# New planner constants in a fused Hyena-and-SwiGLU kernel: block 2's shift taps go to ScalarE, block 3's filter is turned on TensorE, and every engine's order is planned anew

## The chip, the cores and the metric

The kernel runs on one core of one Trainium2 chip. The metric is the device time of one execution in microseconds; the numbers below are medians over runs of the same program. A profile is one more execution, recorded instruction by instruction; its span reaches from the first to the last recorded instruction.

## What is computed

Two layers of the same pair of operators, with weights shared between the layers, on x of 2048 positions by 512 channels in bf16:

```
x = x + A(layernorm(x), k, v);   x = x + B(layernorm(x))     # layer 0
x = x + A(layernorm(x), k, v);   x = x + B(layernorm(x))     # layer 1
A(q, k, v): kv = (sum over j<4 of shift_k[:, j] * k delayed by j) * v
            y  = causal convolution over the 2048 positions of kv with ssm_k, per channel
            return q * (y + ssm_D * kv)
B(x):       (silu(x @ w_gate) * (x @ w_up)) @ w_down          # 512 -> 1792 -> 512
```

The convolution of A depends on k, v and the filters alone, so its result y is the same in both layers and is computed once.

## The kernel before

**Blocks.** The 2048 positions are cut into four blocks of 512 (`NB = 4`); position 4p + r of a block lies on partition p in row r. A block's FFN work is cut into two halves of 256 positions, so there are 16 FFN units, named (layer, block, half): (0,0,0), (0,0,1), (1,0,0), (1,0,1), (0,1,0) and so on to (1,3,1). The convolution is done block by block in the frequency domain: each block of the filter gives a spectrum `H`, `G`, each block of kv a spectrum `X`; products `X[i]*G[j]` are added into `Z[i+j]`, and the inverse of `Z[c]` is `Y[c]`, which block c needs before its layer 0 can begin. Block c therefore needs the products of all blocks up to c.

**One FFN unit (`ffn`).** `zT` holds the normalised input, transposed. For each of 14 chunks of the 1792 columns, TensorE makes a gate and an up product (line 335); two chunks share one PSUM buffer, so a "gate group" or "up group" is eight 256-column matmuls, and there are seven of each in a unit. Four PSUM buffers (`pf`) hold them. ScalarE empties each: SiLU of the gate into `sg` (line 837), a copy of the up into `ht` (line 841). VectorE multiplies the two (line 844), usually two pairs at a time. TensorE then adds the down product into `pd` (line 851, 512 columns, 28 in a unit). At the end ScalarE copies `pd` to `dn` (line 863) and VectorE adds it to x (line 870); units listed in `X_PE` instead add x itself to `pd` by an identity matmul (line 817), and ScalarE writes `pd` straight to x (line 857).

**The step before a unit (`prologue`).** Row statistics come from VectorE's `bn_stats` (lines 706 to 709) or, for the units in `ST1` and `ST2`, from two ScalarE sums per row with `accum_out` (lines 721 and 728, small VectorE steps 724, 732, 734); GpSimd raises the variance to the power -1/2 (`rstd`, line 711 or 736). The normalisation itself is one VectorE `tensor_scalar` per row (line 754) or, for the units in `N_ACT` (the q of A, tile `n`) and `Z_ACT` (the input of B, tile `z`), one ScalarE activation (line 750) behind a small VectorE step (line 743). VectorE then does q*y and x + q*y (lines 776 and 777). Two DMA transposes on SP's queue (line 783) turn `z` into `zT`.

**Convolution steps of one block (`conv`).** The filter block is transposed either on TensorE (`transpose_h`: 16 matmuls with the identity, line 475, and two 1024-column ScalarE copies, line 479) or, for blocks in `H_DMA`, by four ScalarE copies (line 565) and four DMA transposes (line 569). The four shift taps are applied either on TensorE (`shift_mul`: 64 matmuls of 128 columns, four ScalarE copies at line 498, four VectorE products with v at line 499) or, for blocks in `K_ACT`, by `shift_mul_t`: sixteen ScalarE activations with the tap as a per-partition scale (line 578, tiles `ka` and `kc`), three VectorE additions of 2048 columns (line 582), four DMA transposes (line 586) and two VectorE products with v (line 590). The forward transform is eight matmuls with ScalarE copies (line 423) and VectorE butterflies (lines 518 to 531); a product is two VectorE multiplications and one or two additions (lines 635 to 656).

**What sets the order.** Nothing is scheduled by the compiler. `Plan` records each operation with an assumed cost and, where one is given, a due time; `forward` then runs a list schedule over five engines: among the operations that could start first on an engine it takes the one that is due first. The resulting order is written out, engine by engine, and each engine works through its list in that order:

```
key = (max(est, t[e] + self.WAIT[e]), o.due, o.n)
if pick is None or key < pick[0]:
    pick = (key, est, o)
```

FFN operations are due at a place in their unit, counted from `T0` and the list `DUR` of unit lengths; `back` takes `HSL` off the due time of VectorE's steps of the FFN (kind "h") and `ASL` off that of ScalarE's SiLU and copies (kind "a"). Operations of the convolution are due backwards from what needs them, with their costs multiplied by `STRETCH`, and no earlier than `FLOOR`. `SLK` makes the transposes of `z` due earlier. `LOOSE` names the buffer rings whose slots may be handed out in another order than the buffers were declared.

Of the kernel before, what the change touches and what calls it, by code (L numbers as in the profile page):

```python
# [13 lines left out]
ACT = mybir.ActivationFunctionType  # L14
# [2 lines left out]
LN_EPS = 1e-5  # L17

NB = 4
SLK = 8.52  # L20
H_DMA = lambda b: b in {2, 3}
ST1 = lambda l, c, h: (l, c, h) in {(0, 1, 1), (0, 2, 0), (0, 3, 0), (1, 0, 1)}
ST2 = lambda l, c, h: (l, c, h) in {(0, 1, 1), (0, 3, 1), (1, 0, 0)}
ASL = 8.04
K_ACT = lambda b: b in {3}
PASSES = 1
PW = 1.2
PD_ACT, KV_ACT, ST_ACT = True, True, False
HSL = 13.4
Z_ACT = lambda l, c, h: (l, c, h) in {(0, 3, 1), (1, 1, 0), (1, 1, 1)}  # L30
N_ACT = lambda l, c, h: (l, c, h) in {(0, 2, 0), (0, 2, 1), (1, 2, 1), (1, 3, 0), (1, 3, 1)}
Z_DMA = lambda i, j: False
D_DMA = lambda l, c, h: False
X_PE = lambda l, c, h: (l, c, h) in {(0, 3, 1), (1, 1, 0), (1, 2, 0), (1, 3, 1)}
RINGS = {}
T0, FLOOR = 37.71, 9.21
DUR = [20.73, 19.38, 17.95, 16.46, 26.14, 17.1, 26.09, 16.75, 22.3, 20.61, 21.16, 19.35, 17.53, 22.2, 16.85, 27.0]
STRETCH = {1: {"PE": 2.88, "DVE": 1.23, "ACT": 4.33, "POOL": 1.0, "SP": 160.46},
           2: {"PE": 3.08, "DVE": 1.77, "ACT": 1.75, "POOL": 1.0, "SP": 1.07},
           3: {"PE": 3.04, "DVE": 1.08, "ACT": 2.72, "POOL": 1.0, "SP": 1.04}}  # L40
R = 4


# [23 lines left out]
class Plan:  # L67


    LOOSE = ("pc", "ks")  # L70
    WAIT = {"PE": 0.1, "DVE": 0.15, "ACT": 0.1, "POOL": 0.1, "SP": 0.1}
    SAME = {"PE": 0.0, "DVE": 0.06, "ACT": 0.05, "POOL": 0.1, "SP": 0.0}
    CROSS = {"PE": 0.3, "DVE": 0.2, "ACT": 0.25, "POOL": 0.15, "SP": 0.0}
# [60 lines left out]
    def forward(self):  # L134
# [14 lines left out]
        while len(seq) < len(self.ops):  # L149
            best = None  # L150
            for e, cand in ready.items():
                pick = None
                for o in cand:
# [4 lines left out]
                    for b in o.bufs:  # L158
# [4 lines left out]
                        free = sorted(0.0 if s is None else free_at[s] for s in slots[b.ring] if s is None or not todo[s])  # L163
                        if n >= len(free) or (b.ring not in self.LOOSE and qd[heads[b.ring] + n] is not b):
                            ok = False
# [106 lines left out]
def kernel(  # L272
# [192 lines left out]
    def transpose_h(b, ring, order, conv, engs=("ACT",)):  # L465
        hs = new("hs", "hs", [P, R, D], parts=R)
        m = len(engs)
        for r0 in order:
            rows = range(r0, r0 + 2 // m)
            pt = new(ring, "pt", [P, 2 // m, D], BF16)  # L470

            def go(pt=pt, rows=rows):
                for o, r in enumerate(rows):
                    for dt in range(KD):
                        nc.tensor.transpose(pt.t[:, o, dt * P:(dt + 1) * P], hn[b].t[:, dt, r:L:R], ident.t[:])
            add("PE", pe(KD * len(rows), P), go, r=[hn[b], ident], w=[pt], conv=conv, dest=hs)
            sl = slice(rows[0], rows[-1] + 1)
            if engs[order.index(r0) % m] == "ACT":
                add("ACT", act(len(rows) * D), lambda pt=pt, sl=sl: nc.scalar.copy(out=hs.t[:, sl, :], in_=pt.t[:]),
                    r=[pt], w=[(hs, rows)], conv=conv)  # L480
            else:
                add("DVE", tt1(len(rows) * D), lambda pt=pt, sl=sl: nc.vector.tensor_copy(out=hs.t[:, sl, :], in_=pt.t[:]),
                    r=[pt], w=[(hs, rows)], conv=conv)
        return hs
# [50 lines left out]
    def forward4(rows, name, scale, ring, conv):  # L535
        ev = spectrum(name)
        by_residue(rows, ev, scale, ring, ("ACT",), conv)
        return ev
# [8 lines left out]
    def spectrum_h(b, ring="pc"):  # L547
        hs = transpose_h_dma(b) if H_DMA(b) else transpose_h(b, ring, (0, 2), True)
        H[b] = forward4(hs, "H", 2.0 / N, ring, True)
# [11 lines left out]
    def transpose_h_dma(b):  # L561
        hr = new("s8", "hr", [P, R, KD, P], parts=KD)
        hs = new("hs", "hs", [P, R, D], parts=R)
        for dt in range(KD):
            add("ACT", act(D), lambda dt=dt: nc.scalar.copy(
                out=hr.t[:, :, dt], in_=hn[b].t[:, dt, :].rearrange("d (p r) -> d r p", r=R)), r=[hn[b]], w=[(hr, (dt,))],
                conv=True)
        for r in range(R):
            turned[b] = add("SP", 1.25, lambda r=r: nc.sync.dma_start_transpose(
                out=hs.t[:, r].rearrange("p (k f) -> p k f", k=KD), in_=hr.t[:, r]), r=[hr], w=[(hs, (r,))], lat=3.0 if b == 1 else 1.4, conv=True)  # L570
        return hs

    def shift_mul_t(b):

        a, c = new("s8", "ka", [P, 2, R, KD, P], parts=2 * KD), new("s8", "kc", [P, 2, R, KD, P], parts=2 * KD)
        for j, (t, h) in ((3, (a, 0)), (2, (a, 1)), (1, (c, 0)), (0, (c, 1))):
            for dt in range(KD):
                add("ACT", 0.615, lambda j=j, t=t, h=h, dt=dt: nc.scalar.activation(
                    out=t.t[:, h, :, dt], in_=kT[b].t[:, dt, PADL - j:PADL - j + L].rearrange("d (p r) -> d r p", r=R),
                    func=ACT.Copy, scale=tapF.t[:, dt, j:j + 1]), r=[kT[b], tapF], w=[(t, (h * KD + dt,))], conv=True)  # L580
        for t, h in ((a, 1), (c, 0), (c, 1)):
            dve(4 * D, lambda t=t, h=h: nc.vector.tensor_add(out=a.t[:, 0], in0=a.t[:, 0], in1=t.t[:, h]),
                [(t, range(h * KD, h * KD + KD))], [(a, range(KD))], conv=True)
        ks = c
        for r in range(R):
            add("SP", 1.25, lambda r=r: nc.sync.dma_start_transpose(
                out=ks.t[:, 0, r], in_=a.t[:, 0, r]), r=[(a, range(KD))], w=[(c, (r,))], lat=4.0, conv=True)
        for h in range(2):
            sl = slice(2 * h, 2 * h + 2)
            dve(2 * D, lambda sl=sl: nc.vector.tensor_mul(  # L590
                out=vt[b].t[:, sl, :], in0=ks.t[:, 0, sl].rearrange("p r k d -> p r (k d)"), in1=vt[b].t[:, sl, :]),
                [(c, (2 * h, 2 * h + 1))], [(vt[b], (2 * h, 2 * h + 1))], conv=True)

    def spectrum_x(b):
        if K_ACT(b):
            shift_mul_t(b)
        else:
            shift_mul(b, "pc", True, first if b == 1 else ())
        X[b] = butterfly4(forward4(vt[b], f"X{b}", 1.0, "pc", True), True)
# [101 lines left out]
    def ln_stats(c, rows):  # L701
        n = len(rows)
        mv = new("mv", "mv", [P, n, 2], F32, parts=n)
        for o, i in enumerate(rows):
            st = new("st", "bnst", [P, 6], F32)
            add("DVE", 0.6, lambda st=st, i=i: nc.vector.bn_stats(out=st.t[:], in_=xs[c].t[:, i, :]), r=[(xs[c], (i,))], w=[st])  # L706
            add("DVE", 0.09, lambda st=st, o=o: nc.vector.bn_aggr(out=mv.t[:, o, :], in_=st.t[:]), r=[st], w=[(mv, (o,))])
        ve, rstd = new("ve", "ve", [P, n], F32), new("rs", "rstd", [P, n], F32)
        add("DVE", 0.08, lambda: nc.vector.tensor_scalar(out=ve.t[:], in0=mv.t[:, :, 1], scalar1=LN_EPS, scalar2=None,  # L709
                                                         op0=ALU.add), r=[mv], w=[ve])  # L710
        add("POOL", PW, lambda: nc.gpsimd.tensor_tensor(out=rstd.t[:], in0=ve.t[:], in1=nhalf.t[:].to_broadcast((P, n)),  # L711
                                                          op=ALU.pow), r=[ve, nhalf], w=[rstd])
        return mv, rstd
# [46 lines left out]
    def apply_norm(c, h, layer=0):  # L760
        rows = range(HP * h, HP * h + HP)
        st = ln_stats_act(c, rows) if ST1(layer, c, h) else ln_stats(c, rows)
        nmr = shift_of(st, HP) if N_ACT(layer, c, h) else None
        n = new("n", "n", [P, HP, D], parts=HP)
# [4 lines left out]
    def prologue(layer, c, h, on_pe=False):  # L769
# [5 lines left out]
        if not on_pe:  # L775
            dve(HP * D, lambda: nc.vector.tensor_mul(out=n.t[:], in0=n.t[:], in1=y.t[:, sl, :]), [(y, rows)], [n])
            dve(HP * D, lambda: nc.vector.tensor_add(out=x.t[:, sl, :], in0=x.t[:, sl, :], in1=n.t[:]), [n], [(x, rows)])
            st = ln_stats_act(c, rows) if ST2(layer, c, h) else ln_stats(c, rows)
            nmr = shift_of(st, HP) if Z_ACT(layer, c, h) else None
            for o, i in enumerate(rows):  # L780
                z = new("z", "z", [P, D])
                normalise(z, (0,), lambda z=z: z.t[:], c, i, o, st, nmr)
                add("SP", 1.25, lambda z=z, o=o: nc.sync.dma_start_transpose(
                    out=zT.t[:, :, o, :], in_=z.t[:].rearrange("p (k f) -> p k f", k=KD)), r=[z], w=[(zT, (o,))], lat=1.4, slack=SLK)
            return
# [21 lines left out]
    def ffn(unit):  # L807
# [4 lines left out]
        pairs = NF // 2  # L812
        xpe = X_PE(layer, c, h)
        if xpe:
# [157 lines left out]
    for unit in order:  # L972
        start[unit] = t
        t += DUR[order.index(unit)]

# [38 lines left out]

    plan.dues(STRETCH, FLOOR, {u: (start[u], d) for u, d in zip(order, DUR)}, {"h": HSL, "a": ASL})

# [37 lines left out]
```

## Time and profile before

| | us |
|---|---|
| median of 3 runs (357.68 to 358.32) | 358.32 |
| the profiled execution's own time | 358.32 |
| its span | 356.5 |
| TensorE (PE) busy | 347.6 |
| VectorE (DVE) busy | 281.1 |
| ScalarE (ACT) busy | 238.0 |
| GpSimd (POOL) busy | 39.3 |

The profiled execution stands at the median; 1.8 us of it lie outside the span. The granted TensorE clock was 1.00 in every slice. A matmul's busy time overlaps with the next one's, so the cost of an instruction in a packed list is read from the distance between starts in the timeline and not from its mean duration. The same holds, to a smaller degree, for VectorE and ScalarE.

### The profile page before, as it was taken

To read this page: it belongs to the slowest core of one execution; us is meant where nothing else is said; L and a number is where in the kernel's file an instruction comes from. 1 tells how busy PE (TensorE), PEld (TensorE's weight loads), DVE (VectorE), ACT (ScalarE), POOL (GpSimd) and SP (SyncE) were. 2 spreads that over 40 slices of the span, in tenths; PEclk is the share of its full clock that TensorE was granted. 3 is DMA by queue.
4 is the path that set the end of the run, shared out by engine and by line. 5 is a ranking of instruction groups with operands and counts; after the bars stand their busy time and mean duration, and the time that the engine had idled before them with its cause. 6 is when DMAs were issued, how large, how long until landed. Compare 5 with 4: busy or idle time off the path is not lost.

```text
span 356.5 us, 6735 instructions
## 1 busy us (share of the span) xinstructions
PE 347.6 (97%) x2689; PEld 254.4 (71%) x2712; DVE 281.1 (79%) x517; ACT 238.0 (67%) x454; POOL 39.3 (11%) x42
## 2 busy tenths in 40 slices
PE   7999999999999999999999999999999999999996
PEld 6655985867778585868668685858686777768673
DVE  6997999999989999999999999889985323626020
ACT  4587693838878493648878994848484775647352
POOL 1010010130320200111121000201101000101000
PEclk9999999999999999999999999999999999999999
DMA  7999021010241341010311042010103020101000
GB/s 263 306 353 293 2 69 22 0 31 2 45 119 45 63 147 31 0 31 1 79 40 31 1 116 63 2 29 3 31 29 31 30 31 1 31 1 31 30 2 29
DMA packets 37897, 21.98 MB, mean 62 GB/s; under 512 B 29797, under 2 KB 35690, under 8 KB 37866
## 3 DMA queue, kind: packets, MB, share of 16 engines
q1 hardware_dynamic: 37336, 21.03, 22.9%
q10 hardware_dynamic: 530, 0.53, 0.5%
q8 instruction: 21, 0.34, 0.4%
q14 instruction: 10, 0.08, 0.1%
HBM read 12.33 MB, written 2.10 MB: 40 GB/s over the span
## 4 chain that ended last, share of the span: by engine, by line
PE 49%; DVE 35%; ACT 10%; POOL 3%; issue 2%; DMA 1%; ACTq 0%; POOLq 0%; DVEq 0%
PE pf L335 30%; PE pd L851 15%; DVE m L518 4%; DVE ht L844 3%; DVE bnst L706 3%; DVE t L641 3%; DVE t L635 3%; DVE t L651 2%; POOL rstd L736 2%; ACT H L423 2%; DVE Z L656 2%; PE ps L335 2%; PE wm L1020 1%; DVE t L620 1%; DVE Z L648 1%
## 5 line engine op out<-in xcount | busy, mean ns | idle before, releaser
L335 PE MATMUL pf<-zT,wu_sb 128*128 128x256 bf16 x896 | 116.1, 273 | 0.1
L335 PE MATMUL pf<-zT,wg_sb 128*128 128x256 bf16 x896 | 116.1, 273 | 0.0
L335 PEld LDWEIGHTS <-wg_sb 128*128 128x128 bf16 x896 | 87.6, 98 | 18.9 <-issue 0.8
L851 PE MATMUL pd<-wd_sb,ht 128*128 128x512 bf16 x434 | 98.6, 380 | 1.5 <-DVE ht L844 0.8
L335 PEld LDWEIGHTS <-wu_sb 128*128 128x128 bf16 x896 | 87.6, 98 | 11.1
L837 ACT ACTIVATE sg<-pf 128x512 bf16<-128x512 f32 x112 | 68.9, 615 | 18.2 <-PE pf L335 16.7
L851 PEld LDWEIGHTS <-ht 128*128 128x128 bf16 x448 | 43.6, 98 | 49.8 <-DVE ht L844 1.2
L841 ACT CAST ht<-pf 128x512 bf16<-128x512 f32 x112 | 67.3, 601 | 15.0 <-PE pf L335 14.6
L844 DVE TENSOR_TENSOR ht<-ht,sg 128x1024 bf16<-128x1024 bf16 x64 | 39.5, 619 | 25.7 <-ACT ht L841 25.7
L711 POOL TENSOR_TENSOR rstd<-ve,nhalf 128x2 f32<-128x2 f32 x25 | 26.0, 1039 | 203.2 <-DVE ve L709 180.8
L706 DVE BATCH_NORM_STATS2 bnst<-xc 128x6 f32<-128x512 bf16 x50 | 32.5, 685 | 6.2 <-ACT xc L857 5.6
L863 ACT CAST dn<-pd 128x512 bf16<-128x512 f32 x24 | 12.9, 591 | 34.5 <-PE pd L851 34.5
L870 DVE TENSOR_TENSOR xc<-xc,dn 128x1024 bf16<-128x1024 bf16 x12 | 8.2, 686 | 17.8 <-ACT dn L863 17.8
L635 DVE TENSOR_TENSOR t<-X,G 128x2048 bf16<-128x2048 bf16 x18 | 21.9, 1219 | 0.0
L641 DVE TENSOR_TENSOR t<-X,G 128x2048 bf16<-128x2048 bf16 x18 | 21.9, 1217 | 0.0
L736 POOL TENSOR_TENSOR rstd<-ve,nhalf 128x2 f32<-128x2 f32 x7 | 12.0, 1719 | 80.0 <-DVE ve L732 80.0
L423 ACT ACTIVATE X<-ps 128x512 bf16<-128x512 f32 x32 | 18.8, 635 | 1.2 <-PE ps L335 1.1
L423 ACT ACTIVATE H<-ps 128x512 bf16<-128x512 f32 x24 | 13.4, 645 | 4.3 <-PE ps L335 4.3
L656 DVE TENSOR_TENSOR Z<-Z,t 128x2048 bf16<-128x2048 bf16 x12 | 14.7, 1222 | 0.1
L651 DVE TENSOR_TENSOR t<-t,t 128x2048 bf16<-128x2048 bf16 x12 | 14.6, 1221 | 0.1
L335 PE MATMUL ps<-vt,fwd 128*128 128x512 bf16 x54 | 14.4, 380 | 0.1
L335 PEld LDWEIGHTS <-fwd 128*128 128x128 bf16 x96 | 9.3, 98 | 7.2
(95 smaller groups left out, 316.5 us busy)
## 6 DMA issues: line engine op xcount, KB each, us to landing
vt<-in_A_v_dram SPq DMA_DIRECT2D x4, 512.0 KB, 4.6
xc<-in_A_q_dram SPq DMA_DIRECT2D x4, 512.0 KB, 4.8
out_dram<-xc SPq DMA_DIRECT2D x16, 128.0 KB, 1.7
wg_sb<-in_B_w_gate_dram SPq DMA_DIRECT2D x1, 1792.0 KB, 9.2
wu_sb<-in_B_w_up_dram SPq DMA_DIRECT2D x1, 1792.0 KB
wd_sb<-in_B_w_down_dram SPq DMA_DIRECT2D x1, 1792.0 KB, 12.3
hn<-in_A_ssm_k_dram SPq DMA_DIRECT2D x3, 512.0 KB, 7.6
hn<-in_A_ssm_k_dram ACTq DMA_DIRECT2D x1, 512.0 KB, 3.9
```

Source lines behind the costliest of these rows:

```text
L335: nc.tensor.matmul(o, lhsT=lhsT, rhs=rhs, start=(n == 0), stop=(n == len(terms) - 1))
L423: add("ACT", act(D), lambda: nc.scalar.activation(out=view(), in_=ps.t[:], func=ACT.Copy, scale=scale), r=[ps], w=[(buf, keys)], conv=conv)
L635: dve(n * D, lambda t1=t1, part=part: nc.vector.tensor_mul(out=t1.t[:], in0=x.t[:, sl, 0, :], in1=g.t[:, sl, part, :]), [(x, key(slots, (0 ...
L641: dve(n * D, lambda t2=t2, part=part: nc.vector.tensor_mul(out=t2.t[:], in0=x.t[:, sl, 1, :], in1=g.t[:, sl, 1 - part, :]), [(x, key(slots ...
L651: dve(n * D, lambda t1=t1, t2=t2, comb=comb: nc.vector.tensor_tensor(out=t1.t[:], in0=t1.t[:], in1=t2.t[:], op=comb), [t2], [t1], conv=conv)
L656: dve(n * D, lambda t1=t1, part=part: nc.vector.tensor_add(out=z.t[:, sl, part, :], in0=z.t[:, sl, part, :], in1=t1.t[:]), [t1], [zk], con ...
L706: add("DVE", 0.6, lambda st=st, i=i: nc.vector.bn_stats(out=st.t[:], in_=xs[c].t[:, i, :]), r=[(xs[c], (i,))], w=[st])
L711: add("POOL", PW, lambda: nc.gpsimd.tensor_tensor(out=rstd.t[:], in0=ve.t[:], in1=nhalf.t[:].to_broadcast((P, n)), op=ALU.pow), r=[ve, nha ...
L837: add("ACT", act(D), lambda ps=ps, o=o, sg=sg: nc.scalar.activation(out=sg.t[:, o:o + 2, :], in_=ps.t[:], func=ACT.Silu), r=[ps], w=[(sg, ...
L841: add("ACT", act(D), lambda ps=ps, o=o, ht=ht: nc.scalar.copy(out=ht.t[:, o:o + 2, :], in_=ps.t[:]), r=[ps], w=[(ht, (o // 2,))], due=(uni ...
L844: dve(n * W, lambda sg=sg, ht=ht: nc.vector.tensor_mul(out=ht.t[:], in0=ht.t[:], in1=sg.t[:]), [sg], [ht], due=(unit, k / pairs, 0.0, "h"))
L851: nc.tensor.matmul(pds[o].t[:], lhsT=ht.t[:, q, o * P:(o + 1) * P], rhs=wt["d"].t[:, ft, :], start=(ft == 0 and not xpe), stop=(ft == NF - 1))
```

## The change

Only constants change; the functions stay as they are.

```diff
-SLK = 8.52
-H_DMA = lambda b: b in {2, 3}
-ST1 = lambda l, c, h: (l, c, h) in {(0, 1, 1), (0, 2, 0), (0, 3, 0), (1, 0, 1)}
-ST2 = lambda l, c, h: (l, c, h) in {(0, 1, 1), (0, 3, 1), (1, 0, 0)}
-ASL = 8.04
-K_ACT = lambda b: b in {3}
+SLK = 12.82
+H_DMA = lambda b: b in {2}
+ST1 = lambda l, c, h: (l, c, h) in {(0, 3, 0), (0, 3, 1), (1, 0, 1), (1, 1, 0), (1, 1, 1), (1, 3, 0)}
+ST2 = lambda l, c, h: (l, c, h) in {(0, 2, 0), (0, 2, 1), (1, 2, 0)}
+ASL = -36.81
+K_ACT = lambda b: b in {2, 3}
...
-HSL = 13.4
-Z_ACT = lambda l, c, h: (l, c, h) in {(0, 3, 1), (1, 1, 0), (1, 1, 1)}
-N_ACT = lambda l, c, h: (l, c, h) in {(0, 2, 0), (0, 2, 1), (1, 2, 1), (1, 3, 0), (1, 3, 1)}
+HSL = 60.24
+Z_ACT = lambda l, c, h: (l, c, h) in {(0, 1, 0), (0, 1, 1), (0, 2, 0), (1, 0, 0), (1, 0, 1), (1, 2, 0), (1, 2, 1), (1, 3, 0)}
+N_ACT = lambda l, c, h: (l, c, h) in {(0, 3, 0), (1, 0, 0)}
...
-X_PE = lambda l, c, h: (l, c, h) in {(0, 3, 1), (1, 1, 0), (1, 2, 0), (1, 3, 1)}
+X_PE = lambda l, c, h: (l, c, h) in {(0, 1, 0), (0, 2, 1), (0, 3, 0), (1, 0, 1), (1, 3, 1)}
 RINGS = {}
-T0, FLOOR = 37.71, 9.21
-DUR = [20.73, 19.38, 17.95, 16.46, 26.14, 17.1, 26.09, 16.75, 22.3, 20.61, 21.16, 19.35, 17.53, 22.2, 16.85, 27.0]
-STRETCH = {1: {"PE": 2.88, "DVE": 1.23, "ACT": 4.33, "POOL": 1.0, "SP": 160.46},
-           2: {"PE": 3.08, "DVE": 1.77, "ACT": 1.75, "POOL": 1.0, "SP": 1.07},
-           3: {"PE": 3.04, "DVE": 1.08, "ACT": 2.72, "POOL": 1.0, "SP": 1.04}}
+T0, FLOOR = 87.92, 19.78
+DUR = [20.67, 16.0, 19.32, 17.95, 26.57, 16.97, 27.0, 19.26, 27.0, 17.51, 19.02, 23.16, 25.1, 27.0, 18.4, 23.39]
+STRETCH = {1: {"PE": 1.0, "DVE": 1.41, "ACT": 1.84, "POOL": 1.0, "SP": 58.52},
+           2: {"PE": 1.2, "DVE": 1.44, "ACT": 1.78, "POOL": 1.0, "SP": 1.0},
+           3: {"PE": 6.31, "DVE": 1.15, "ACT": 2.46, "POOL": 1.0, "SP": 3.85}}
...
-    LOOSE = ("pc", "ks")
+    LOOSE = ()
```

In the instruction lists of the two programs this comes to the following counts (before to after):

- TensorE: shift matmuls of 128 columns 192 to 128; filter transposes of 128 columns 32 to 48; identity matmuls of 512 columns (line 817) 8 to 10.
- VectorE: additions of 2048 columns at line 582 3 to 6; products with v at line 590 2 to 4 and at line 499 8 to 4; `bn_stats` and its aggregate 50 to 46 each, line 709 25 to 23; lines 724, 732 and 734 7 to 9 each; line 743 8 to 10; normalisations at line 754 48 to 44; additions at line 870 12 to 11.
- ScalarE: taps 16 to 32; copies at line 498 8 to 4, at line 565 8 to 4, of 1024 columns at line 479 2 to 4; sums at lines 721 and 728 14 to 18 each; normalisations at line 750 16 to 20; the copies of `pd` (lines 857 and 863) stay 32 together.
- SP: DMA transposes at line 569 8 to 4 and at line 586 4 to 8. The load of block 2's v now stands behind the first pair of `zT` transposes, and the transposing load of block 3's k (line 367) stands directly ahead of block 2's four transposes at line 586.

The order of the lists is unchanged up to the first shift matmuls of block 1, some 35 us into the execution, and differs from there on. All 64 shift matmuls of block 1 now come before the first gate group. In ScalarE's list block 2's taps stand as ten in a row, then three, then three; block 3's as eleven, two and three (before: eight in a row, then one at a time). The last down matmuls of unit (1,0,1) now stand behind the first gate group of unit (0,1,0).

## The prediction

> **What bounds the kernel now.** First the page's busy table and its slices of time, to see which engine is full where.
>
> ```profile
> PE 347.6 (97%) x2689; PEld 254.4 (71%) x2712; DVE 281.1 (79%) x517; ACT 238.0 (67%) x454; POOL 39.3 (11%) x42
> ...
> PE   7999999999999999999999999999999999999996
> DVE  6997999999989999999999999889985323626020
> ACT  4587693838878493648878994848484775647352
> PEclk9999999999999999999999999999999999999999
> ```
>
> TensorE is full from slice 2 to slice 39, at full clock. VectorE is as full for two thirds of the span and then empties. The same by stretches, columns PE, PEld, DVE, ACT, POOL:
>
> ```profile
> 37.00:230.00 193.00, 191.50 (x1499) 142.51 (x1509) 186.83 (x315) 141.14 (x279) 26.34 (x19) 1.00 0.18 43
> 230.00:280.00 50.00, 49.79 (x361) 35.45 (x363) 38.62 (x74) 29.55 (x58) 5.05 (x6) 1.00 0.13 22
> 280.00:353.00 73.00, 72.79 (x554) 54.23 (x555) 24.36 (x55) 41.92 (x78) 4.06 (x5) 1.00 0.09 19
> ```
>
> Until 230 us two engines are packed at once; after that TensorE alone. Busy time hides idle inside overlapping matmuls, so I read start distances in the timeline, here around block 3's taps:
>
> ```profile
> 195.94 5.99 PE L851 MATMUL pd<-wd_sb,ht 128*128 128x512 bf16 x27
> 197.76 5.41 ACT L578 ACTIVATE ka<-kTb,tapF 128x512 bf16<-128x512 bf16 x8
> 201.77 1.04 PE L335 MATMUL pf<-zT,wg_sb 128*128 128x256 bf16 x8
> 202.64 1.04 PE L335 MATMUL pf<-zT,wu_sb 128*128 128x256 bf16 x8
> 203.05 1.07 ACT L863 CAST dn<-pd 128x512 bf16<-128x512 f32 x2
> 204.39 1.04 PE L335 MATMUL pf<-zT,wu_sb 128*128 128x256 bf16 x8
> 204.66 0.63 ACT L837 ACTIVATE sg<-pf 128x512 bf16<-128x512 f32 x1
> 205.33 1.03 PE L335 MATMUL pf<-zT,wg_sb 128*128 128x256 bf16 x8
> ```
>
> A group of eight costs TensorE 202.64 - 201.77 = 0.87 us (0.109 a matmul), a 512-column matmul 0.216 (28 down matmuls fill 195.72 to 201.77), a 128-column one about 0.056 (16 in 0.9). Its whole list: 1792 x 0.109 + 608 x 0.216 + 308 x 0.056 = 343.9 us, and its last matmul ends at 352.8. So all its waiting is 8.9 us, 6.9 of it before unit (0,0,1) starts at 59.77, where the list sums to 52.9. I call this difference an engine's lag: TensorE's is 7.7 when (1,0,1) starts (101.51) and 8.8 when (0,2,1) starts (220.39) and at the end. Summed likewise, VectorE's lag is 5.2 at (0,0,1)'s z (ends 51.20, list 46.0) and 8.2 at (0,2,0)'s (193.07, list 184.9): 3 us of waiting in 140.
>
> The timeline also shows what a row of taps costs: eight taps hold ScalarE for 203.05 - 197.76 = 5.29 us (0.661 each). The gate group that began at 201.77 is emptied only at 204.66, and the third gate group, which wants its PSUM buffer, starts at 205.33 instead of 205.26. The 28 down matmuls beside the taps were the cover. With two later gaps, block 3's taps cost TensorE 0.36 us.
>
> **TensorE's list.** Minus 64 shift matmuls (3.58), plus 16 filter transposes (0.90), plus two identity matmuls (0.43): 2.25 us shorter. This lies wholly on the path, and it is all that the change can take off, apart from the 1.9 us of waiting after 59.77.
>
> **VectorE's list.** Plus three additions (3 x 1.135) and two products (2 x 0.60), minus four products at line 499 (4 x 0.34), four bn_stats with aggregates (4 x 0.76), four normalisations (4 x 0.35), one addition (0.67) and some small steps: about 1.1 us shorter, nothing by itself.
>
> **ScalarE's list.** Plus 16 taps (10.6), eight row sums (5.4), four normalisations (2.9), two wide copies (1.8), minus eight copies (4.1): 16.6 us longer, on an engine with 118 us free. Whether it costs anything depends on where it stands. GpSimd has two more of its slow powers and stays a tenth busy.
>
> On price, the groups of one normalisation in both places (last columns: busy, mean ns of one):
>
> ```profile
> L754 DVE TENSOR_SCALAR z<-xc,mv,rstd 128x512 bf16<-128x512 bf16 x26 | 9.6, 408 | 3.7 <-POOL rstd L711 3.2 <-POOL rstd L736 0.6
> L750 ACT ACTIVATE z<-xc,nmr,rstd 128x512 bf16<-128x512 bf16 x6 | 4.6, 807 | 1.9 <-DVE nmr L743 1.9
> ```
>
> The work costs twice as much where it goes. [...]
>
> **Burst 1: block 2's ten taps, late in unit (1,0,1).** Count from TensorE's start of the gate group (call it a) whose SiLU stands ahead of the taps. ScalarE begins that SiLU at 1.1 (in the trace a group is picked up 1.1 us after its start) and the taps at 1.6, ends them at 8.2, and copies up a by 8.8. TensorE meanwhile has up a, gate b, up b, gate c (to 4.4) and 18 matmuls of 512 columns (to 8.2); up c needs up a's buffer and waits 0.7. Then come gate d, and at 10.6 the down matmuls that read the product of pairs a and b. Copy b ends at 9.8, so the product could end at 10.5; but VectorE's list, at a lag of 5.6 to 6 (that of the trace less the waits for rstd that the new order covers), ends it only at 11.6: 1.1 more. The product of pair c and gate f's buffer add 0.25 each. Sum 2.3; bounds 0.7 (ScalarE alone) and 4.0 (VectorE's lag still 7.4). I take 2.3, the walk itself.
>
> **Burst 2: block 3's eleven taps, as unit (0,2,1) begins.** Count from the start of the last up group of (0,2,0). ScalarE copies it by 1.6, has taps until 8.9, two copies of pd until 9.8, two taps until 11.15, then SiLU, done at 11.75. TensorE has 28 down matmuls (to 6.9) and four groups (to 10.4): the third gate group waits 1.4, a later one 0.15. Together 1.6, against 0.36 before.
>
> **Through VectorE.** Unit (0,2,1) started 16 us after its z ended (204.34) before. The new order puts 12.5 us more VectorE work ahead of that z, and a product read by (0,2,0)'s down matmuls 3.0 us of TensorE list ahead of (0,2,1) ends at 209.5 of VectorE's list. At the lag of before (8.0) this allows the unit to start at 209.5 + 8.0 + 0.35 + 3.0 = 220.85. Any further lag e adds in full. After burst 1, TensorE (lag 7.3 + 2.3 = 9.6; 7.3 because the 0.65 wait for a product at 78 us has no counterpart) ends an up group at 142.5 of its list, at 152.1; with the copy, 0.95, VectorE gets the product at 153.05. At the old lag of 7.8 its list would be there at 151.3. So e is about 1.7.
>
> **The sum.** (0,2,1) starts at the later of 209.8 + 9.6 + 1.6 = 221.0 (TensorE) and 220.85 + 1.7 = 222.55 (VectorE), 2.16 later than before. From there TensorE's list is 0.44 shorter (two transform matmuls now stand ahead of the unit), and it was packed. 358.32 + 2.16 - 0.44 = 360.0 us. The profiled execution stands at the median, so nothing is corrected.
>
> **Transfers moved.** Block 2's v waits behind two transposes but landed at some 55 us for a use after 110; nothing. On SP's queue block 3's k now stands ahead of the four transposes of line 586, and the queue was held by such a load for
>
> ```profile
> 5.89 10.20 SPq L367 DMA_TRANSPOSE kTb<-in_A_k_dram  x1
> ...
> 27.08 6.93 SPq L367 DMA_TRANSPOSE kTb<-in_A_k_dram  x1
> ...
> 120.03 2.87 SPq L367 DMA_TRANSPOSE kTb<-in_A_k_dram  x1
> ```
>
> The first two ran beside the weights. At 2.87, like the third, VectorE has 7 us of other list between the last addition and the first product with v, against 2.9 + 2.5 + 1.2: covered. At 6.93 VectorE waits about 3.6.
>
> **Rivals.** (1) The list alone decides: if both bursts are covered (products ready when the down matmuls come, ScalarE's queue short), TensorE gains its 2.25 us and up to 1.3 of old waits: 355 to 356.5, about 356.1. For it: TensorE's waits were that small before. Against: the ten taps stand between two PSUM copies and 6.6 us exceeds the cover. It decides if the two bursts cost under 1.5 us together. Chance 0.15. (2) VectorE keeps up (e at or below 0) and only the bursts count: 221.0, so 358.5. For it: ten z normalisations leave VectorE, against six of n that come back, and its waits for rstd go. Chance 0.2. (3) The k load holds SP's queue for 6.9 us in front of block 2's transposes; VectorE, packed, passes the 3.6 on: 361 to 364. Against: no other traffic then. Chance 0.1. My forecast, 359.0 to 361.2, has 0.55. That the taps do not move is excluded by the instruction lists.
>
> **Numbers.** Below 0.2% (0.7 us) this measurement tells nothing from no change. Rival 1 and a sliver make faster 0.16; most of rival 2, same 0.2; the rest, slower 0.64. The range goes from rival 1's upper half (357.2) to rival 3's lower half (362.2).
>
> **What would show it.** TensorE's waits should total about 4 us more than before after 110 us, at up c and the down matmuls beside block 2's taps and at the third gate group of (0,2,1); VectorE should wait for products around 152 us; TensorE should be packed from (0,2,1) on. If TensorE shows no gap beside the taps, the walk is wrong; if it does and VectorE still arrives early, only the VectorE step is.

## The result, and the profile after

The change made the kernel slower: 362.56 us (median of 4 runs, 361.33 to 363.2) against 358.32 (median of 4, 357.68 to 358.32), a ratio of 1.0119 with a 95% interval of 1.0088 to 1.0149. The forecast was 360.0, with a range of 357.2 to 362.2: the direction was right, the size was not. The profiled execution took 362.23 us, its span is 360.5.

The page after, the lines that answer to those shown of before (busy table, then the span in 40 slices):

```profile
PE 347.0 (96%) x2640; PEld 252.4 (70%) x2666; DVE 280.9 (78%) x511; ACT 253.9 (70%) x484; POOL 41.3 (11%) x42
...
PE   7899999999999999999999789999999999999996
...
DVE  6997999999999995999999999799966250637020
ACT  4578684759879977739777994976687555746361
...
PEclk9999999999999999999999989999999999999999
```

ScalarE has its 16 us more, as forecast, and the other two are unchanged in sum. New are three marks: TensorE's 7 in slice 23 (198 to 207 us), the granted clock's 8 in slice 24 (207 to 216 us), and VectorE's 5 in slice 16 (135 to 144 us). By stretches (the stretch, its length, then the busy time of PE, PEld, DVE, ACT and POOL, and the granted clock):

```profile
37.00:230.00 193.00, 187.15 (x1413) 137.13 (x1426) 184.44 (x304) 149.48 (x289) 26.69 (x18) 0.99 0.19 43
230.00:280.00 50.00, 49.84 (x375) 36.79 (x376) 39.10 (x77) 37.11 (x79) 6.40 (x6) 1.00 0.10 22
280.00:357.00 77.00, 76.74 (x574) 56.47 (x577) 26.16 (x57) 41.98 (x77) 4.38 (x5) 1.00 0.08 18
```

All the loss is ahead of 230 us: TensorE is busy for 187.2 of 193 us there, where it was for 191.5. The timeline at the start of unit (0,2,0) holds most of it. Columns: start, length, engine, line, operation; in brackets the idle time ahead and what ended it:

```profile
191.72 0.67 ACT L841 CAST ht<-pf 128x512 bf16<-128x512 f32 x1
...
192.29 2.13 POOL L736 TENSOR_TENSOR rstd<-ve,nhalf 128x2 f32<-128x2 f32 x1 [11.20 <-DVE ve L732]
...
193.97 1.04 PE L335 MATMUL pf<-zT,wu_sb 128*128 128x256 bf16 x8
...
194.65 1.52 ACT L750 ACTIVATE z<-xc,nmr,rstd 128x512 bf16<-128x512 bf16 x2 [2.27 <-DVE nmr L743]
...
197.51 0.59 ACT L841 CAST ht<-pf 128x512 bf16<-128x512 f32 x1
197.98 5.44 ACT L578 ACTIVATE ka<-kTb,tapF 128x512 bf16<-128x512 bf16 x8
...
203.32 2.05 ACT L578 ACTIVATE kc<-kTb,tapF 128x512 bf16<-128x512 bf16 x3
...
204.03 1.04 PE L335 MATMUL pf<-zT,wu_sb 128*128 128x256 bf16 x8
...
205.28 1.04 ACT L863 CAST dn<-pd 128x512 bf16<-128x512 f32 x2
...
206.22 1.40 ACT L578 ACTIVATE kc<-kTb,tapF 128x512 bf16<-128x512 bf16 x2
...
207.53 0.57 ACT L837 ACTIVATE sg<-pf 128x512 bf16<-128x512 f32 x1
...
208.15 1.86 PE L335 MATMUL pf<-zT,wg_sb 128*128 128x256 bf16 x8 [3.08 <-ACT sg L837]
...
209.80 0.68 DVE L844 TENSOR_TENSOR ht<-ht,sg 128x1024 bf16<-128x1024 bf16 x1
209.81 1.67 PE L335 MATMUL pf<-zT,wu_sb 128*128 128x256 bf16 x8
```

Read ScalarE's lines first. After the copy at 191.72 it stood still for 2.27 us: the next in its list were two normalisations of `z` (line 750), which need VectorE's `nmr`, which needs GpSimd's `rstd` (192.29, 2.13 us long). Two SiLUs and two copies stand behind them, and only then come thirteen taps. The first SiLU of the unit therefore starts at 207.53, and TensorE's third gate group, due at 204.91, starts at 208.15. And then its groups of eight last 1.66 and 1.50 us from start to start instead of 0.87: the clock.

```profile
204.90:208.10 3.20, 0.16 (x2) 0.00 (x0) 3.17 (x7) 3.20 (x7) 1.53 (x1) 0.93 0.00 0
208.10:211.30 3.20, 3.15 (x16) 2.22 (x16) 3.17 (x7) 3.20 (x6) 0.00 (x0) 0.53 0.44 127
```

In the 3.2 us behind the wait the granted clock is 0.53 (third value from the right). Summed as before, by start distances beyond what each matmul takes (those above 0.04 us), TensorE loses:

| TensorE's waits after 37 us | before | after | forecast for after |
|---|---|---|---|
| up to 103 us | 1.12 | 1.73 | about 0.5 |
| beside block 2's taps, 116 to 125 us | 0 | 1.13 | 2.3 |
| 178 to 199 us | 0.61 | 0.76 | 0.6 |
| beside block 3's taps | 0.36 | 3.25 | 1.6 |
| half clock behind that | 0 | 1.41 | 0 |
| sum | 2.09 | 8.28 | |

8.28 - 2.09 - 2.25 (the shorter list) = 3.94, and the two profiled executions differ by 3.91. So the account closes; what it does not say is whether taking a wait away would give its time back. That is what the runs are for.

### The profile page after: what moved, and what is told of

Same layout as the page of the kernel before. It is cut to its first block, busy times and chain, and to the rows that moved or that the text cites. A ratio compares the mean times of both kernels' runs of the same rounds, so it can differ in the third digit from the quotient of the medians.

```text
span 360.5 us, 6661 instructions
## 1 busy us (share of the span) xinstructions
PE 347.0 (96%) x2640; PEld 252.4 (70%) x2666; DVE 280.9 (78%) x511; ACT 253.9 (70%) x484; POOL 41.3 (11%) x42
## 4 chain that ended last, share of the span: by engine, by line
PE 55%; DVE 26%; ACT 14%; issue 2%; POOL 1%; DMA 1%; ACTq 0%; POOLq 0%; DVEq 0%
PE pf L335 34%; PE pd L851 16%; PE ps L335 4%; ACT ka L578 3%; DVE bnst L706 3%; DVE t L635 2%; DVE m L518 2%; DVE t L641 2%; DVE ht L844 2%; ACT sg L837 2%; ACT H L423 2%; ACT ht L841 1%; DVE t L620 1%; DVE Z L656 1%; ACT X L423 1%
## 5 line engine op out<-in xcount | busy, mean ns | idle before, releaser
L851 PE MATMUL pd<-wd_sb,ht 128*128 128x512 bf16 x433 | 99.7, 379 | 1.2 <-DVE ht L844 0.3
L711 POOL TENSOR_TENSOR rstd<-ve,nhalf 128x2 f32<-128x2 f32 x23 | 27.8, 1208 | 175.2 <-DVE ve L709 161.4
L863 ACT CAST dn<-pd 128x512 bf16<-128x512 f32 x22 | 11.7, 585 | 28.8 <-PE pd L851 28.8
L706 DVE BATCH_NORM_STATS2 bnst<-xc 128x6 f32<-128x512 bf16 x46 | 29.9, 685 | 0.5
L736 POOL TENSOR_TENSOR rstd<-ve,nhalf 128x2 f32<-128x2 f32 x9 | 12.3, 1362 | 109.8 <-DVE ve L732 109.8
L728 ACT ACTIVATE jk<-xc,nm 128x512 bf16<-128x512 bf16 x18 | 13.4, 746 | 3.9 <-DVE nm L724 3.8
L750 ACT ACTIVATE z<-xc,nmr,rstd 128x512 bf16<-128x512 bf16 x16 | 12.2, 816 | 5.5 <-DVE nmr L743 5.5
L857 ACT CAST xc<-pd 128x512 bf16<-128x512 f32 x10 | 5.3, 587 | 15.2 <-PE pd L851 15.2
```

The costliest lines, as they stand in the source:

```text
L728: add("ACT", 0.71, lambda jk=jk, o=o, i=i: nc.scalar.activation(out=jk.t[:], in_=xs[c].t[:, i, :], func=ACT.Square, bias=nm.t[:, o:o + 1], ...
L851: nc.tensor.matmul(pds[o].t[:], lhsT=ht.t[:, q, o * P:(o + 1) * P], rhs=wt["d"].t[:, ft, :], start=(ft == 0 and not xpe), stop=(ft == NF - 1))
```

## Experiments

The first eight keep the order of every list and change only what their edit says; a helper (in all of them but the one with eight taps less, which edits the kernel's own lines) takes the planner's five lists, applies `edit`, and writes them out, so that line numbers in those kernels are up to 97 higher. `o.emit = lambda: None` leaves a step out: its time is gone, its result is missing, and the rest stands as it was. Kernel before in the same sessions: 357.61 to 357.75 us (medians). The changed kernel was timed in the first session alone, and its four executions lie 1.9 us apart: a difference of under 1 us from its 362.56 shows nothing.

Theories. **A**: ScalarE's row of taps alone sets the start of unit (0,2,1). **B**: the row sets it, and VectorE's last products stand 1.3 us behind. **C** (the step through VectorE of the prediction): VectorE alone sets it. Formed after the first three runs, **D**: two rows stand side by side at the start of (0,2,0), ScalarE's taps and VectorE's steps between the last product of one unit and the first of the next, and each alone holds TensorE.

**Two additions less.** Lines 656 at 195.8 and 217.9 us are left out.

```diff
+    for o in [o for o in lists["DVE"] if _names(o) == ["t1", "Z"]][7:9]:
+        o.emit = lambda: None
```

> Leaves out two of VectorE's additions into Z (line 656, at 195.8 and 217.9 us of the changed kernel; 2 x 1.135 = 2.27 us of its list), so the products of unit (0,2,0) and the z of (0,2,1) come earlier. Theory A (ScalarE's row of taps alone sets the start of unit (0,2,1)): no change, 362.6 us, (0,2,1) still at 224.8. Theory B (two queues: the row of taps sets it, and VectorE's last products stand 1.3 us behind it): no change either, 362.6. Theory C (VectorE alone sets it, as the step through VectorE had it): (0,2,1) 2.3 us earlier, 360.3.

Measured: 362.47 us (362.29 to 363.5). No change: C is out for these late steps.

**Eight taps less.** Block 3's `kc` half is left out.

```diff
-                add("ACT", 0.615, lambda ...: nc.scalar.activation(
+                add("ACT", 0.615, lambda ...: None if t is c and b in LESS else nc.scalar.activation(
...
-            ... nc.vector.tensor_add(out=a.t[:, 0], in0=a.t[:, 0], in1=t.t[:, h])
+            ... nc.vector.tensor_add(out=a.t[:, 0], in0=a.t[:, 0], in1=a.t[:, 1] if b in LESS else t.t[:, h])
```

> Leaves out eight of block 3's sixteen taps on ScalarE (the kc half; the additions that took them read the second half of ka again, so VectorE's list is unchanged); five of them stand ahead of the first SiLU of unit (0,2,0): 3.3 us. Theory A: the 3.25 us wait at the third gate group goes and with it the 1.4 us at half clock, so 4.6 us less: about 357.9, (0,2,1) at 220.1. Theory B: the wait and the low clock go too, but VectorE's product still ends at 220.4 and 3.0 us of TensorE's list follow it, so (0,2,1) starts at 223.5, 1.3 us earlier: about 361.2, with new waits of TensorE for VectorE's products. Theory C: no change, 362.6.

Measured: 362.71 us (361.77 to 363.67). Five taps fewer ahead of the SiLU, and nothing gained: A and B both fail. The timeline of this run says why:

```profile
204.28 0.64 ACT L839 ACTIVATE sg<-pf 128x512 bf16<-128x512 f32 x1
...
204.97 1.03 PE L336 MATMUL pf<-zT,wg_sb 128*128 128x256 bf16 x8
...
207.59 1.04 PE L336 MATMUL pf<-zT,wu_sb 128*128 128x256 bf16 x8
...
209.86 0.68 DVE L846 TENSOR_TENSOR ht<-ht,sg 128x1024 bf16<-128x1024 bf16 x1
...
210.60 1.04 PE L853 MATMUL pd<-wd_sb,ht 128*128 128x512 bf16 x4 [1.97 <-DVE ht L846]
...
211.18 0.63 ACT L723 ACTIVATE jk<-xc 128x512 bf16<-128x512 bf16 x1 [4.80 <-DVE xc L779]
...
211.81 0.58 ACT L839 ACTIVATE sg<-pf 128x512 bf16<-128x512 f32 x1
...
212.44 1.86 PE L336 MATMUL pf<-zT,wg_sb 128*128 128x256 bf16 x8 [0.80 <-ACT sg L839]
```

The SiLU is done at 204.9 and the third gate group starts on time, at 204.97. Then the down matmuls wait 1.97 us for the unit's first product, which VectorE starts at 209.86: where it stood in the changed kernel (209.80), behind the rest of H3's butterfly, two steps of G3, statistics, an addition of a tap and a normalisation. ScalarE itself waits 4.80 us for VectorE's `xc` (a row sum stands ahead of the next SiLU), and TensorE 0.80 for that. The clock fell here too. By stretches (clock third from the right):

```profile
208.20:211.50 3.30, 1.33 (x8) 0.54 (x7) 3.27 (x7) 0.32 (x1) 0.00 (x0) 1.00 0.38 123
211.60:218.40 6.80, 6.00 (x26) 3.52 (x25) 6.70 (x10) 5.33 (x14) 1.49 (x1) 0.50 0.49 92
```

It was down by 211.6 us, behind the idle time of 1.97 us (208.63 to 210.60) and before the one of 0.80 (up to 212.44) had passed, and stayed at 0.50 until 218.4.

**Both.**

> Both: eight of block 3's taps and two of VectorE's additions left out. Theory A: as with the taps alone, 357.9. Theory B: more than the two alone together (0 and 1.3): the product ends at 218.1, (0,2,1) starts at 220.1 to 221.2, 3.6 to 4.6 us less, 358.0 to 359.0. Theory C: as with the additions alone, 360.3.

Measured: 361.95 us (361.84 to 362.12), 0.6 less than the changed kernel, which is within the spread of that kernel's own executions: no clear gain, and far from B's 358.0 to 359.0. Of the two additions only the one at 195.8 stands ahead of the product that TensorE waited for. This gave D, and the next pair shortens the right row.

**VectorE's row shorter.** Three steps between the two products are left out.

```diff
+    i = dve.index(pick(dve, "ka")[3])
+    dn = [o for o in dve[:i] if _names(o) == ["dn", "xc"]][-1]
+    mul = [o for o in dve[i:] if _names(o) == ["Yk", "n"]][0]
+    for o in (dn, dve[i], mul):
+        o.emit = lambda: None
```

> Leaves out three of VectorE's steps between the last product of unit (1,1,1) and the first of unit (0,2,0): the addition of dn (line 870), the first addition of block 3's taps (line 582) and the multiplication of n by Yk (line 776), 0.60 + 1.135 + 0.60 = 2.34 us, so that this product ends at 208.1 instead of 210.4; ScalarE's row of taps stands as it was. Theory D (two rows side by side, ScalarE's of 10.1 us and VectorE's of 11.7 us, each of which alone holds TensorE at the start of (0,2,0)): no change, 362.5, as ScalarE's row still holds the third gate group. Theory V (VectorE alone is late): 2.3 us less and no low clock, 358.8 to 360.2.

Measured: 362.45 us (360.83 to 362.73). No change, as D has it; that VectorE's row alone holds the unit (V) fails. In its profiled execution TensorE still waits for the SiLU as long as in the changed kernel (3.08 there), but at a clock of 1.00 throughout:

```profile
207.92 1.03 PE L393 MATMUL pf<-zT,wg_sb 128*128 128x256 bf16 x8 [3.07 <-ACT sg L895]
```

**Both rows shorter.** The same edit and eight taps less.

> The same three steps and eight of block 3's taps left out. Theory D: TensorE's waits of 3.25 us for ScalarE and of 2.13 + 0.96 us for VectorE (those of the run with eight taps less) both go, and with them the low clock: about 4.7 us less than the changed kernel, 357.9 to 358.5, (0,2,1) starts at about 220.1. Theory V: no more than with VectorE's row alone. Any theory in which something else holds (0,2,1), the clock or the transposes of z: over 360.

Measured: 359.26 us (358.89 to 359.92), 3.3 less than the changed kernel, with the clock at 1.00 and (0,2,1) starting at 221.71 instead of 224.77. The waits of TensorE that are left between 196 and 225 us (us in total, times, longest):

```profile
PE pf L394 <- ACT sg L897: 0.8, 1, 0.8
PE pd L911 <- DVE ht L904: 0.7, 2, 0.4
```

Taps alone +0.15, VectorE's row alone -0.1, both -3.3: that is two holds side by side, and D stands. Part of the 3.3 is the low clock, a mean of 0.995 in three of the changed kernel's four executions and 0.998 to 1.000 here: against the changed kernel's one execution at full clock (361.33) it is 2.1. The gain is 0.8 to 1.4 us less than D's: counted by start distances, 0.57 us of TensorE's wait for the first product and 0.96 for a SiLU behind the row sum, which still waits for `xc`, are left.

**VectorE's idle time at 135 to 140 us.** VectorE idled there where it had not before:

```profile
137.47 0.43 DVE L844 TENSOR_TENSOR ht<-ht,sg 128x512 bf16<-128x512 bf16 x1 [2.65 <-ACT ht L841]
...
139.70 1.23 DVE L518 TENSOR_TENSOR m<-X 128x2048 bf16<-128x2048 bf16 x1 [1.80 <-ACT X L423]
```

Theory **E** is that this is handed on in full, as the prediction said of any lag. The run leaves out as much VectorE work behind it.

```diff
+    subs = [o for o in lists["DVE"] if _names(o) == ["t2", "t1"]]
+    adds = [o for o in lists["DVE"] if _names(o) == ["t1", "Z"]]
+    for o in subs[4:6] + adds[4:6]:
+        o.emit = lambda: None
```

> Leaves out four of VectorE's steps on products (lines 651 and 656) between 147 and 161 us, 4 x 1.135 = 4.54 us: as much as VectorE idles at 135 to 140 us in the changed kernel (2.65 + 1.80 us, for a copy and for X2's spectrum) and did not in the one before. Theory E (this idle time is passed on in full to (0,2,1), as the step through VectorE said of any further lag): everything behind it 4 us earlier, 358 to 359. Theory D: VectorE soon waits again for copies and sums that TensorE and ScalarE make, so it is no earlier at 198 us; only the z normalisation ahead of the taps may come up to 0.9 us earlier: 361.5 to 362.5, or 1.4 us less if that keeps the clock up.

Measured: 361.85 us (360.27 to 362.41), 0.7 less, within the spread, for 4.54 us of work. E is out. VectorE's list is tied again and again to copies and sums of the other engines, and what it saves at 150 us it mostly spends waiting: between 142 and 200 us it is idle for 5.10 us where it was for 1.85 in the changed kernel, so 3.25 of the 4.54 us are gone again.

**The price of a wait.** In the kernel before, at (0,3,1), where TensorE alone is the bound, the first SiLU is done 13 and 5 times more.

```diff
+    silu = pick(lists["ACT"], "pf", "sg")[7 * 13]
+    once = silu.emit
+    silu.emit = lambda: [once() for _ in range(1 + STALL)]
```

> The kernel before, with the first SiLU of unit (0,3,1) done 13 times more on ScalarE, where TensorE alone is the bound: 13 x 0.48 = 6.2 us, of which 1.75 are covered by the groups that TensorE has still to do (the third gate group of (0,3,1) starts 3.5 us after the unit, the SiLU was done 1.75 after it). Theory W (a wait costs what it lasts): 4.5 us more, 362.8, granted clock 1.00 throughout. Theory W+C (a wait of over 3 us is followed by some 3 us at half clock, as after the 3.25 us wait of the changed kernel): 5.9 us more, 364.2, with a slice of lower clock behind the wait.

Measured: 366.03 us (365.88 to 366.53), 8.3 more than before. Each repeat took 0.62 us and not 0.48, so the wait was 6.41 us; the other 1.9 are the clock:

```profile
296.70:300.20 3.50, 3.50 (x33) 3.12 (x32) 2.36 (x6) 3.17 (x6) 0.00 (x0) 1.00 0.00 0
...
306.70:310.20 3.50, 3.50 (x17) 2.47 (x17) 0.76 (x2) 3.00 (x6) 0.00 (x0) 0.50 0.00 0
310.40:313.00 2.60, 2.60 (x26) 2.34 (x24) 2.37 (x4) 1.78 (x4) 0.00 (x0) 1.00 0.00 0
```

The same 3.5 us hold 33 matmuls ahead of the wait and 17 behind it. The clock fell at 303.6 us, in the middle of the wait, and rose at 310.4; only the 3.7 us of it behind the wait cost anything, at half speed 1.9.

> The kernel before with the first SiLU of unit (0,3,1) done five times more. The run with 13 more gave TensorE a wait of 6.41 us, so eight fewer, 0.60 us each, leave 1.6 us. Theory W (no price but the wait): 359.4. If even this wait is followed by half clock: 1.5 us more, 360.9, granted clock 0.995.

Measured: 359.0 us (358.81 to 359.26), 1.3 more, for a wait of 1.38 us, at a mean clock of 0.999 to 1.000. So this wait cost about what it lasted.

**One stretch in another order.** All work is kept, TensorE's list too; 98 steps of VectorE, ScalarE and SP between 180 and 232 us change places, most by a few positions. The order came from a search over moves that keep dependencies and buffers, with the durations of these traces (a tap 0.66 us where the planner's cost says 0.615).

```diff
+ORDER = {"PE": "...", "DVE": "...", "ACT": "...", "POOL": "...", "SP": "..."}
...
-        plan.issue(*plan.order(PASSES), T0, warm)
+        plan.issue(*rearranged(plan, *plan.order(PASSES)), T0, warm)
```

> All work kept. Only the order of VectorE's, ScalarE's and SP's steps between about 180 and 232 us is changed (98 of them moved), so that the two rows at the start of unit (0,2,0) are broken up; TensorE's list is untouched. Theory D (two rows side by side hold TensorE): the 3.25 us wait, its low clock and the waits for VectorE's products go; as with both rows shorter, 358.0 to 359.5, (0,2,1) starts at about 221. Rival (VectorE and ScalarE simply have too much to do there, whatever the order): 361.5 to 362.6.

Measured: 358.89 us (358.23 to 359.36), 3.7 less than the changed kernel, ratio to before 1.003 (1.002 to 1.004). ScalarE now does the last SiLUs and copies of (1,1,1), with its first two taps among them, before the `z` normalisations, in the time that it had spent waiting, so that the last of these copies ends at 196.66 and not at 198.10; and it puts the last taps between the copies and SiLUs of (0,2,0):

```profile
192.73 0.85 ACT L669 ACTIVATE ka<-kTb,tapF 128x512 bf16<-128x512 bf16 x1
...
194.81 0.89 ACT L669 ACTIVATE ka<-kTb,tapF 128x512 bf16<-128x512 bf16 x1
...
195.96 0.70 ACT L932 CAST ht<-pf 128x512 bf16<-128x512 f32 x1
196.43 1.65 ACT L841 ACTIVATE z<-xc,nmr,rstd 128x512 bf16<-128x512 bf16 x2
...
204.76 0.70 ACT L928 ACTIVATE sg<-pf 128x512 bf16<-128x512 f32 x1
205.25 0.87 ACT L669 ACTIVATE kc<-kTb,tapF 128x512 bf16<-128x512 bf16 x1
```

TensorE waits 0.48 us for that SiLU instead of 3.25. So the work fits there; its order did not.

**All lists in another order.** The same search over the whole of both kernels behind 40 us, with slack, so that a step that takes longer than planned holds nobody up (**S**: the split of the work is good, the order costs; **R**: the split overloads ScalarE and VectorE).

> All work of the changed kernel, on the engines where it put it; all five lists rearranged behind 40 us so that no engine's steps stand in front of something that TensorE is about to need, with slack left for longer steps. Theory S (the split of the work among the engines is good for the 2.25 us that TensorE's list is shorter; what costs is the order): TensorE's waits after 37 us fall from 8.3 us to 1 to 2, so 355 to 357.5, faster than the kernel before. Rival R (the split itself overloads ScalarE and VectorE): over 359.

> The kernel before, rearranged in the same way: all its work on the engines where it was. TensorE waits 2.1 us there after 37 us, which is all that can go: 356.0 to 358.0. By theory S about 2 us slower than the changed kernel rearranged; by rival R faster than that.

> The changed kernel rearranged as in the run before last, but with less slack left for longer steps. If the slack is not needed: the same 355 to 357.5 or up to 0.6 us less. If it is: TensorE's waits come back at the places where VectorE or ScalarE is late, 357 to 359.

| | us | ratio to before, 95% interval | TensorE's waits after 37 us |
|---|---|---|---|
| changed kernel rearranged | 355.23 | 0.9929 (0.9916 to 0.9941) | 1.26 |
| the same, less slack | 354.92 | 0.9923 (0.9911 to 0.9936) | 1.40 |
| before rearranged | 356.54 | 0.9965 (0.9952 to 0.9979) | 0.19 |

S stands. With its waits gone the changed kernel is 1.3 to 1.6 us faster than the one before treated alike, and both are faster than the kernel before. (Less slack was not tried on the kernel before; it had 0.19 us of waits left to gain.) In the first of them VectorE's idle time at 135 to 140 us has shrunk to

```profile
135.45 0.43 DVE L941 TENSOR_TENSOR ht<-ht,sg 128x512 bf16<-128x512 bf16 x1 [0.23 <-ACT ht L938]
136.05 2.36 DVE L615 TENSOR_TENSOR m<-X 128x2048 bf16<-128x2048 bf16 x2 [0.18 <-ACT X L520]
```

## Why the prediction was wrong, point by point

**TensorE's list, 2.25 us shorter: right.** The account above closes with it, and the rearranged kernels show that it can be had.

**ScalarE's 16.6 us and the prices: right.** The page shows 253.9 against 238.0, and a `z` normalisation still costs twice as much there (last columns: busy, mean ns of one):

```profile
L750 ACT ACTIVATE z<-xc,nmr,rstd 128x512 bf16<-128x512 bf16 x16 | 12.2, 816 | 5.5 <-DVE nmr L743 5.5
...
L754 DVE TENSOR_SCALAR z<-xc,mv,rstd 128x512 bf16<-128x512 bf16 x16 | 5.9, 409 | 1.7 <-POOL rstd L711 1.7
```

The idle column of the first line is what the prediction passed over: moved to ScalarE, the step makes ScalarE wait for VectorE and GpSimd, 5.5 us in all.

**Burst 1, 2.3 us: too large, 1.13.** The wait of up c was 0.56 where the walk had 0.7. The product of pairs a and b, 1.1 in the walk, cost nothing:

```profile
118.16 0.69 DVE L844 TENSOR_TENSOR ht<-ht,sg 128x1024 bf16<-128x1024 bf16 x1 [0.16 <-ACT ht L841]
...
118.96 1.89 PE L851 MATMUL pd<-wd_sb,ht 128*128 128x512 bf16 x8
```

VectorE waited 0.16 us for copy b, so it was earlier there than the lag of 5.6 to 6 that the walk gave it, and the product ended at 118.85, ahead of the down matmuls. The product of pair c cost 0.36 and gate f's buffer 0.21, where the walk had 0.25 each.

**Burst 2, 1.6 us: the step that failed, by two terms.** The walk let ScalarE finish its copy of the last up group "by 1.6" after that group's start. It finished at 198.10, 4.1 after 193.97, because the two normalisations of `z` and their 2.27 us of idle time stand ahead of the last SiLUs and copies. The rest of the walk, from there to the SiLU, holds: 10.1 us counted, 10.0 measured. So the wait was 3.25 and not 1.4. The run with one stretch in another order agrees: there the last copy ended 2.05 after the start of its group, the taps were spread, and 0.48 of the wait was left. The second term was not in the sum at all: the 1.41 us at half clock behind the wait. The text also names the place one unit late: the row stands at the start of (0,2,0), behind the last up group of (1,1,1).

**Through VectorE, 222.55 for the start of (0,2,1): wrong in its rule, though VectorE mattered.** The extra lag did come, but at 135 to 140 us, not at 152, 4.45 us and not 1.7: 2.65 for the copy of an up group, and 1.80 for X2's spectrum, which waits for block 2's taps, transposes and products and which the walk did not follow. It is not added in full, as the run with four steps less shows. Where VectorE did hold TensorE, as long as ScalarE's row was shortened, was the first product of (0,2,0); the step looked only at the last ones. Taking the later of two ends, as the sum did, was the right form: with two holds side by side, each of them taken away alone shows a gain of nothing. But both stand at the start of (0,2,0), 205 to 210 us, and the sum looked for VectorE's some 10 us later.

**From (0,2,1) on: right.** 0.44 less was forecast; 132.80 us before and 132.37 after from there to the last matmul make 0.43. The sum missed by 2.2 us at that one point (224.77 against 222.55); the other 0.3 is what the profiled execution lies below the median.

**Rivals.** (1) The list alone decides: not so in this order, but its 356.1 was within 1.2 us of what the rearranged kernels reach. (2) VectorE keeps up and only the bursts count: half right. TensorE did not wait for VectorE between 199 us and (0,2,1), but the bursts, the low clock included, came to more than its 358.5, and VectorE's row at (0,2,0) stood ready behind ScalarE's. (3) The k load holds SP's queue, 361 to 364 us; the measured 362.56 lies in this range by luck:

```profile
123.06 2.40 SPq L367 DMA_TRANSPOSE kTb<-in_A_k_dram  x1
125.56 5.33 SPq L586 DMA_TRANSPOSE kc<-ka  x4
```

it held it 2.40 us, and as VectorE's last addition of taps ended only at 124.9, the transposes lost 0.7 us and VectorE none: its products with v, at 131.80 and 134.14, did not wait. **Transfers.** One effect was missed: unit (1,0,1) waited 0.8 us at 100.4 us for its `zT`, whose transposes now stand right behind a 512 KB load of the filter on SP's queue; with it the waits up to 103 us came to 1.73 where about 0.5 was forecast. That the load delays them was not tried by itself.

**What would show it.** Of the signs, TensorE's gaps beside the taps and its packed list from (0,2,1) on came true. Its waits after 110 us grew by 5.6 us, 1.41 of them at half clock, and not by about 4; and VectorE waited at 135 to 140 us, not around 152.

## What to carry to other kernels

When work moves to an engine with time to spare, walk that engine's list from the last step that the bound engine needs back to the first one that waits for somebody else: a normalisation that waits for statistics holds everything behind it (here for 2.27 us), and the walk must start there. When taking a wait away gains nothing, don't conclude that it cost nothing: shorten the second engine's row between the same two hand-overs too, and compare the two alone with both together. A static order with waits of 8 us in it says little on the split of the work; break up the rows that stand in front of the bound engine, with measured durations, before the split is judged.

## What the runs showed of the hardware

In the kernel before with SiLUs repeated, TensorE's wait of 1.38 us cost 1.3 us, at a mean clock of 0.999 to 1.000 in all six executions; the wait of 6.41 us cost 8.3, at 0.991 in all four, with 3.7 us at a granted clock of 0.50 behind it. In between the length alone did not decide. Of the four executions of the changed kernel (wait 3.25 us in the one that was traced) three had a mean clock of 0.995 and took 362.23 to 363.2 us, one had 1.000 and took 361.33. With VectorE's row shorter, the traced execution has the same wait, 3.07 us idle, and kept 1.00; the other three had 0.994 to 0.995. With eight taps less the clock fell behind an idle time of 1.97 us. The granted clock then stood at 0.50 for 3.4 us (207.7 to 211.1 in the changed kernel) or for 6.8 (211.6 to 218.4 with eight taps less, 303.6 to 310.4 with thirteen SiLUs more). What decides whether and when it falls was not shown; no run moved a wait to try it.
